# One core: a step's product P moved ahead of its first feed-forward piece, feed-forward input rows read where they were written, guard squares in halves

## Chip, core and metric

The kernel runs on one core of a Trainium2 chip. The metric is the device time of one execution in microseconds (us), median of several runs. A core has five engines that run side by side, each in the order of its own program: TensorE (PE: matmuls into PSUM; PEld is its weight load), VectorE (DVE), ScalarE (ACT), GpSimd (POOL) and SyncE (SP, which here only issues DMAs). They wait for each other through semaphores.

## What is computed

```python
def _attn_ref(r, k, v, w, a, b):          # (4, 8, 768, 40) each: batch, heads, time, width
    state = zeros((B, H, D, D)); y = zeros_like(r)
    for t in range(S):
        y[:, :, t] = einsum('bhd,bhde->bhe', rt, state)
        Sa = einsum('bhde,bhe->bhd', state, at)
        state_decay = state * wt[:, :, None, :] - einsum('bhd,bhe->bhde', Sa, bt)
        state = state_decay + einsum('bhd,bhe->bhde', vt, kt)
    return y

def _moe_ref(x, w_in, w_out):             # x: (3072, 320), w_in: (320, 2048), w_out: (2048, 320)
    r = maximum(x @ w_in, 0.0)
    return (r * r) @ w_out
```

`rt`, `wt` and so on are the rows of time t. The output of the first part, with its heads laid side by side, is the input x of the second. So: a recurrence over 768 time steps for 32 heads of width 40, and a feed-forward layer of 2048 behind it.

## The kernel before

**Tiling.** The recurrence is turned into matmuls over chunks of 128 time steps: 6 chunks (`NCH`), 4 batches (`NB`), 4 pairs of heads a batch (`PB`). One *step* `st` of the main loop handles two pairs (four heads) of one chunk; 8 steps make a chunk (`NQ`), 48 the whole (`NS`), and the loop has two more to drain. Two steps with consecutive numbers, even and odd, share one batch `m`. Steps of a chunk with q = 0 to 3 and 4 to 7 are the two halves (`hf`) of a chunk.

**One step** works on two steps' data at a time, since the results of step st-1 are finished in step st. In its order on TensorE:
- `st_ex_mm(st-1)` (tile ex) and `st_a_mm(st+1)` (tile ca);
- `st_z(st-1)` (tile uy, part from the state of the chunk before, through UBD);
- `st_p(st)` (tile P): ScalarE copies it out as Mc (`st_m`); `st_corr` multiplies Mc back into P, VectorE forms c (`st_c1`), `st_corr` again, and ScalarE writes the result into EVX (`st_sn`, line 296), followed by the guard square jk; GpSimd forms x and Cc;
- `st_t(st, st-2)` (tile tb): transposes that result (VectorE copies it to SnT) and a piece of the next chunk's state (ScalarE copies it to UBD);
- `st_kb(st-1)` fills uy, which `st_y` turns into the output rows YS and the state UZ in the next step.

P and tb have one PSUM buffer between them (tag `sp`, one buffer), so P of a step cannot be written before both SnT and UBD of the step before have been read out of tb.

**Preparations** of a batch m (casts, the decay cs with GI and Gp, and transpositions t1, t2, t3 with their copies RV, KBT, GT and AT) hang in slots of the loop: `prepare(st, 1)` and `prepare(st, 4)`. Even steps have GT and AT of one batch and lnW and the casts of another in slot 1, and cs, GI, Gp, Kp, Bp in slot 4; odd steps RV in slot 1 and KBT in slot 4. `prepare(st, 5)` issues the loads of a batch, six DMAs on SP. Preparations end with step 44; UBD is written for steps 2 to 41.

**Feed-forward.** Each half chunk gives 256 rows of x. `gather` collects them from YS (two heads to a column block, head 2p in partitions 0 to 39 and head 2p+1 in 64 to 103) into three tiles X of 120, 120 and 80 partitions, with eight DMAs. Then there are 12 *pieces*: eight `ffn_in` (two of the 16 blocks of 128 hidden units each: six matmuls into hp, a Relu on ScalarE to hs, a square on VectorE or GpSimd to Gt) and four `ffn_out` (eight matmuls each into an op tile, two pieces to an output tile osb). `filler(st)` runs one piece at each of three places in a step, when it is due; the last ones run behind the loop. hp, op, t1, t2, t3 and cs share two PSUM buffers (tag `ff`).

**Guards.** Squares of some tiles are summed into ACC (jk each step; jm twice at the end of a chunk, over Mc and Cc). If a sum is out of bounds, a slow general path at the end is taken; here it isn't.

**Order.** Each engine's order is the order in which the code calls it; nothing reorders it. The loop body up to the last filler:

```python
filler(st)
if st >= 2:
    st_y(st - 2)
if 1 <= st <= NS:
    st_ex_ev(st - 1)
    st_z(st - 1)
if st < NS:
    st_p(st)
    st_m(st)
prepare(st, 1)
```

Of the kernel before, what the change touches and what calls it, by code (L numbers as in the profile page):

```python
# [7 lines left out]
FP32 = mybir.dt.float32  # L8
BF16 = mybir.dt.bfloat16
# [9 lines left out]
def kernel(  # L19
# [68 lines left out]

    NACC = NS + 2 * NCH + 2 * NBC
    AN, AM, AC, AG, AI = 0, NS, NS + NCH, NS + 2 * NCH, NS + 2 * NCH + NBC
    ACC = gl.tile([128, NACC], FP32, name="ACC")
    ones_f = gl.tile([128, 128], FP32, name="ones_f")
    nc.gpsimd.memset(ones_f[:], 1.0)
# [196 lines left out]
    def st_sn(st):  # L292
        c, q = divmod(st, NQ)
        P, EVX, c1, CN = Ps.pop(st), EVXs[st % NEV], c1s.pop(st), CNs.pop(st)
        Sn = EVX[:, :, :, L + LV:2 * LV].rearrange("p i s e -> p (i s) e")
        nc.scalar.activation(out=Sn, in_=P[:].rearrange("p i s e -> p (i s) e")[:, :, 0:D],  # L296
                             func=ACTF.Copy, scale=-1.0)
        t_ = qdp.tile([128, 4, D], FP32, name="x1", tag="x1")
        nc.gpsimd.tensor_tensor(out=t_[:], in0=Mc[c][:, q], in1=c1[:], op=ALU.add)  # L299
        nc.gpsimd.tensor_tensor(out=Cc[c][:, q], in0=t_[:], in1=Sn, op=ALU.add)  # L300
        jk = qdp.tile([128, 2, 2, L], BF16, name="jk", tag="jk", bufs=1)
        nc.scalar.activation(out=jk[:], in_=CN[:, :, :, 1, :], func=ACTF.Square,  # L302
                             accum_out=ACC[:, AN + st:AN + st + 1])
        if q == NQ - 1:
            for src, at in ((Mc.pop(c), AM), (Cc.pop(c), AC)):
                jm = qdp.tile([128, NQ, 4, D], BF16, name="jm", tag="jm", bufs=1)
                nc.scalar.activation(out=jm[:], in_=src[:], func=ACTF.Square,  # L307
                                     accum_out=ACC[:, at + c:at + c + 1])

    def st_t(st, su):  # L310
        tb = ps.tile([128, 4, 128], BF16, name="tb", tag="sp")
# [61 lines left out]
    def st_y(st):  # L373
        c, o, j0, p2, EVX = where(st)
        uy = uys.pop(st)
        if st % NQ == 0:
            YSs[c] = chp.tile([128, NP, L], BF16, name="YS", tag="YS")
        nc.vector.tensor_tensor(out=YSs[c][:, p2, :], in0=uy[:, :, 0:L],  # L378
                                in1=o.GT[:, j0:j0 + 2, 0:L], op=ALU.mult)
        if c + 1 < NCH:  # L380
            gl_ = o.GT[:, j0:j0 + 2, L:L + 1]
            for u in range(2):
                nc.vector.tensor_tensor(
                    out=UZs[(c + 1) % 2][half(u), p2, 64 * u:64 * u + D],
                    in0=uy[half(u), :, L:LV],
                    in1=gl_[half(u)].to_broadcast([64, 2, D]), op=ALU.mult)

    Xs, Gts, WIN = {}, {}, []  # L390
    rows = [3 * D, 3 * D, 2 * D]
    WOUT = gl.tile([128, NJ, DM], BF16, name="WOUT")
    for g in range(3):
        WIN.append(gl.tile([128, DFF], BF16, name=f"WIN{g}"))

    def load_win():
        off = 0
        for g in range(3):
            nc.gpsimd.dma_start(out=WIN[g][0:rows[g], :], in_=moe_w_in[off:off + rows[g], :])
            off += rows[g]  # L400

    def load_wout():
        nc.gpsimd.dma_start(out=WOUT[:], in_=moe_w_out.rearrange("(j p) f -> p j f", p=128))

    def gather(c, hf, engines):
        X = Xs[c, hf] = [chp.tile([128, HB, L], BF16, name=f"X{g}", tag=f"X{g}")
                         for g in range(3)]
        for h in range(NHH):
            g, row, s = h // 3, (h % 3) * D, h % 2
            src = YSs[c][64 * s:64 * s + D].rearrange("e (b p) t -> e b p t", b=NB)  # L410
            engines[h % len(engines)].dma_start(
                out=X[g][row:row + D], in_=src[:, HB * hf:HB * hf + HB, h // 2, :])

    later = []

# [4 lines left out]
    def ffn_in(c, hf, jj):  # L420
        flush()
        if jj == 0:
            Gts[c, hf] = chp.tile([128, NJ, HB, L], BF16, name="Gt", tag="Gt")
        hp = ps.tile([128, 2, HB * L], FP32, name="hp", **where_ff())
        for u in range(2):
            j = 2 * jj + u
            for g in range(3):
                nc.tensor.matmul(out=hp[:, u, :], lhsT=WIN[g][0:rows[g], j * 128:(j + 1) * 128],  # L428
                                 rhs=Xs[c, hf][g][0:rows[g]].rearrange("p a b -> p (a b)"),
                                 start=(g == 0 and u == 0), stop=(g == 2),  # L430
                                 skip_group_check=True)
        hs = ffp.tile([128, 2 * HB * L], BF16, name="hs", tag="hs")
        nc.scalar.activation(out=hs[:], in_=hp[:].rearrange("p u x -> p (u x)"), func=ACTF.Relu)  # L433
        eng = nc.gpsimd if jj % 2 and not tail else nc.vector
        Gt = Gts[c, hf]
        later.append(lambda: eng.tensor_tensor(  # L436
            out=Gt[:, 2 * jj:2 * jj + 2].rearrange("p j a b -> p (j a b)"),
            in0=hs[:], in1=hs[:], op=ALU.mult))
# [27 lines left out]
    def filler(st):  # L466
        if fill and fill[0][0] <= st:
            fill.pop(0)[1]()
# [8 lines left out]
    def prepare(st, lot):  # L477
        for f, m in when.pop((st, lot), []):
            f(m)
# [6 lines left out]
    for st in (-2, -1):  # L486
        prepare(st, 1)
        prepare(st, 4)
    nc.gpsimd.memset(UZs[1][:], 0.0)
    for st in range(NS + 2):  # L490
        if 1 <= st <= NS:
            st_ex_mm(st - 1)
        if st + 1 < NS:
            st_a_mm(st + 1)
        filler(st)
        if st >= 2:
            st_y(st - 2)
        if 1 <= st <= NS:
            st_ex_ev(st - 1)
            st_z(st - 1)  # L500
        if st < NS:
            st_p(st)
            st_m(st)
        prepare(st, 1)
        if st < NS:
            st_corr(st, Mc[st // NQ][:, st % NQ], False)
            st_c1(st)
        if st + 1 < NS:
            st_a_ev(st + 1)
        filler(st)  # L510
        if st < NS:
            st_corr(st, c1s[st], True)
            st_sn(st)
        filler(st)
        prepare(st, 4)
        st_t(st, st - 2)
        if 1 <= st <= NS:
            st_kb(st - 1)
        if st == 1:
            load_win()  # L520
        if st == 4:
            load_wout()
        if st >= 2:
            c, q = divmod(st - 2, NQ)
            hf = q // (NQ // 2)
            if q % (NQ // 2) == NQ // 2 - 1:
                gather(c, hf, [nc.sync] if st < NS + 1 else [nc.sync, nc.gpsimd, nc.sync])
                at = st + (3 if c + 1 < NCH else 2)
                fill += [(at, lambda c=c, hf=hf, j=j: ffn_in(c, hf, j)) for j in range(NJ // 2)]
                fill += [(at, lambda c=c, hf=hf, b_=b_, p_=p_: ffn_out(c, hf, b_, p_))  # L530
                         for b_ in range(HB) for p_ in range(2)]
        prepare(st, 5)
        if st == 3:
            nc.gpsimd.memset(UZs[0][:], 0.0)
# [9 lines left out]
    nc.vector.memset(ok[:], 1.0)  # L544
    nc.vector.tensor_scalar(out=ok[:, AN:AN + NS], in0=es[:, AN:AN + NS], scalar1=0.75,
                            scalar2=None, op0=ALU.is_le)
    nc.vector.scalar_tensor_tensor(out=ok[:, AM:AM + NCH], in0=es[:, AM:AM + NCH],
                                   scalar=2.0 ** -16, in1=es[:, AC:AC + NCH],
                                   op0=ALU.mult, op1=ALU.is_ge)
    nc.vector.tensor_scalar(out=ok[:, AG:NACC], in0=es[:, AG:NACC], scalar1=2.0 ** 100,  # L550
                            scalar2=None, op0=ALU.is_le)
# [19 lines left out]
    def general():  # L571
# [36 lines left out]
        for bb in range(NB):  # L608
            with tc.For_i(0, T, L) as t0:
                xg = fb.tile([128, NHH, D], FP32, name="xg")  # L610
                nc.sync.dma_start(
                    out=xg[:], in_=ydr[bb, :, bass.ds(t0, L), :].rearrange("h t e -> t h e"))
                xT = fb.tile([128, 3, L], BF16, name="xT")
                xf = xg[:].rearrange("p h e -> p (h e)")
                hp = ps.tile([128, L], FP32, name="hp", tag="ff", bufs=2)
                for g in range(3):
                    nc.tensor.transpose(out=hp[0:rows[g], :],
                                        in_=xf[:, 3 * D * g:3 * D * g + rows[g]], identity=IDf[:])
                    nc.vector.tensor_copy(out=xT[0:rows[g], g, :], in_=hp[0:rows[g], :])
                gt = fb.tile([128, NJ, L], BF16, name="gt")  # L620
                hs = fb.tile([128, L], BF16, name="hb")
                for j in range(NJ):
                    for g in range(3):
                        nc.tensor.matmul(out=hp[:], lhsT=WIN[g][0:rows[g], j * 128:(j + 1) * 128],
                                         rhs=xT[0:rows[g], g, :], start=(g == 0), stop=(g == 2))
                    nc.scalar.activation(out=hs[:], in_=hp[:], func=ACTF.Relu)
                    nc.vector.tensor_tensor(out=gt[:, j, :], in0=hs[:], in1=hs[:], op=ALU.mult)
                op_ = ps.tile([128, DM], FP32, name="op_", tag="ff", bufs=2)
# [39 lines left out]
```

## Time and profile before

| | |
|---|---|
| median of 3 runs | 330.63 us (330.14 to 330.99) |
| the profiled execution | 330.49 us, its span 328.8 us |
| busy in the span: PE, PEld, DVE, ACT, POOL | 280.4, 213.3, 222.7, 232.8, 188.3 us |
| mean granted clock of TensorE | 0.943 |
| first-layer matmuls (L428) | 576, mean 275 ns |
| hs, Relu of 128x512 on ScalarE (L433) | 96, mean 597 ns |
| jm, square of 128x1280 on ScalarE (L307) | 12, mean 1264 ns |
| X from YS (L411) | 96 DMAs of 20 KB, 93 on SP and 3 on GpSimd |
| WIN from HBM (L399) | 3 DMAs on GpSimd, 6.3 us (two) and 9.5 us to landing |
| WOUT from HBM (L403) | 1 DMA on GpSimd, 13.3 us to landing |

The span is what lies between the first and the last instruction of the profiled execution; 1.7 us of its time lie around it. A step's beginning can be read off the first matmul of ex: steps 1 to 9 begin at 25.07, 30.06, 34.90, 38.72, 44.54, 49.81, 54.77, 58.59 and 67.47 us, step 17 at 115.54, 25 at 163.50, 33 at 211.47, 41 at 259.43 and 48 at 296.97. The last eight first-layer pieces start at 310.21.

Timeline rows below show: start, duration, engine and line, operation, output<-inputs and shape, number of instructions merged, and in brackets the idle time of the engine before them with what ended it. The ends of matmuls are modelled; starts are what can be relied on, so spacings from one start to the next are used.

### The profile page before, as it was taken

Reading aid. Unit: us, or ns where it says so; the run is one execution under the profiler, and the core shown is the slowest. Engines: PE = TensorE matmul, PEld = TensorE weight load, DVE = VectorE, ACT = ScalarE, POOL = GpSimd, SP = SyncE. Lnnn points to the kernel's source line nnn. Section 1 sums busy time; section 2 is a strip of 40 time slices with the busy share of each in tenths; the row PEclk is TensorE's granted clock in tenths of the full one; section 3 lists DMA queues with packets and bytes.
Section 4 is the critical chain, followed back from the end, with each engine's and each line's share of the span. In section 5 each row is a group of like instructions: output and inputs, shape, how many; then the busy total and the mean of one; then the engine's idle time right before and its main releaser. Section 6 shows DMA issues by size and latency. Waiting matters only on the chain.

```text
span 328.8 us, 10009 instructions
## 1 busy us (share of the span) xinstructions
PE 280.4 (85%) x3856; PEld 213.3 (65%) x3856; DVE 222.7 (68%) x545; ACT 232.8 (71%) x569; POOL 188.3 (57%) x342
## 2 busy tenths in 40 slices
PE   4478777799999799999799999899998899888990
PEld 3446555577777577777577777677776677666770
DVE  7226968587787587786686886686876775954430
ACT  3366766886886986887986787886887886538450
POOL 3367757296585485676476676476674673533300
PEclk9555978899999999999999999999999999999997
DMA  8992999985737437635736844735862701000100
GB/s 136 174 165 40 176 165 167 169 126 99 151 71 138 94 69 141 126 69 112 128 55 121 147 82 78 144 62 120 131 106 47 147 18 44 20 23 28 55 22 29
DMA packets 164187, 32.86 MB, mean 100 GB/s; under 512 B 158660, under 2 KB 163780, under 8 KB 164130
## 3 DMA queue, kind: packets, MB, share of 16 engines
q1 hardware_dynamic: 161586, 29.44, 49.7%
q0 software_dynamic: 2544, 2.68, 5.1%
q8 instruction: 32, 0.52, 0.7%
q14 instruction: 25, 0.20, 0.2%
HBM read 28.84 MB, written 3.93 MB: 100 GB/s over the span
## 4 chain that ended last, share of the span: by engine, by line
PE 56%; ACT 18%; issue 7%; DVE 7%; POOL 4%; DMA 3%; SPq 3%; ACTq 0%; DVEq 0%; POOLq 0%
PE hp L428 12%; PE t L197 6%; PE ex L341 4%; PE P L280 4%; PE cs L179 4%; ACT hs L433 3%; ACT jm L307 3%; PE uy L368 3%; ACT RV L204 3%; SPq L81 3%; PE tb L316 3%; PE ca L242 2%; DMA NV<-in_v_dram 2%; DVE c L288 2%; ACT GT L224 2%
## 5 line engine op out<-in xcount | busy, mean ns | idle before, releaser
L428 PE MATMUL hp<-X,WIN 120*128 120x256 bf16 (+1 forms) x576 | 78.9, 275 | 8.1 <-ACT osb L458 6.1
L433 ACT ACTIVATE hs<-hp 128x512 bf16<-128x512 f32 x96 | 57.3, 597 | 26.1 <-PE hp L428 22.7
L349 DVE TENSOR_TENSOR EVX<-ex,MEX 128x512 bf16<-128x512 f32 x96 | 61.8, 686 | 1.7 <-PE ex L341 0.5
L428 PEld LDWEIGHTS <-WIN 120*128 120x128 bf16 (+1 forms) x576 | 50.7, 98 | 18.9 <-issue 9.6
L250 DVE TENSOR_TENSOR CN<-ca,MCN 128x512 bf16<-128x512 f32 x96 | 61.4, 681 | 0.7 <-PE ca L242 0.7
L299 POOL TENSOR_TENSOR x<-Mc,c 128x160 f32<-128x160 bf16 x48 | 23.3, 486 | 66.7 <-DVE c L288 66.6
L436 POOL TENSOR_TENSOR Gt<-hs 128x512 bf16<-128x512 bf16 x43 | 48.4, 1125 | 9.9 <-ACT hs L433 9.6
L454 PEld LDWEIGHTS <-Gt 128*128 128x128 bf16 x384 | 34.3, 97 | 13.4 <-POOL Gt L436 0.8
L280 PEld LDWEIGHTS <-CN 128*128 128x128 bf16 x384 | 23.2, 98 | 27.2 <-issue 23.6
L326 DVE COPY SnT<-tb 128x256 bf16<-128x256 bf16 x48 | 14.0, 291 | 33.3 <-PE tb L322 27.6
L300 POOL TENSOR_TENSOR Cc<-x,EVX 128x160 bf16<-128x160 f32 x48 | 25.3, 527 | 17.1 <-ACT EVX L296 16.8
L436 DVE TENSOR_TENSOR Gt<-hs 128x512 bf16<-128x512 bf16 x53 | 27.4, 519 | 9.4 <-ACT hs L433 9.2
L225 DVE TENSOR_TENSOR AT<-t,GT 128x512 bf16<-128x512 bf16 x24 | 10.2, 425 | 31.4 <-ACT GT L224 31.4
L302 ACT ACTIVATE jk<-CN 128x512 bf16<-128x512 bf16 x48 | 30.1, 627 | 0.0
L212 ACT ACTIVATE KBT<-t 128x1024 bf16<-128x1024 bf16 x24 | 24.6, 1024 | 6.0 <-PE t L197 6.0
L204 ACT ACTIVATE RV<-t 128x1024 bf16<-128x1024 bf16 x24 | 24.6, 1023 | 5.1 <-PE t L197 3.0
L188 POOL TENSOR_TENSOR Kp<-NK,GI 128x320 bf16<-128x320 f32 x24 | 22.4, 933 | 6.6 <-ACT GI L182 5.6
L280 PE MATMUL P<-c,CN 128*128 128x40 bf16 x192 | 12.4, 181 | 13.5 <-DVE c L288 13.5
L288 DVE TENSOR_TENSOR c<-P,Mc 128x160 bf16<-128x160 f32 x48 | 15.3, 319 | 10.4 <-PE P L280 9.6
L378 DVE TENSOR_TENSOR YS<-uy,GT 128x256 bf16<-128x256 f32 x48 | 20.2, 421 | 1.2 <-PE uy L368 0.8
L242 PE MATMUL ca<-AT,KBT 64*128 64x128 bf16 x384 | 20.0, 228 | 1.2 <-DVE AT L225 1.2
L296 ACT ACTIVATE EVX<-P 128x160 bf16<-128x160 f32 x48 | 14.4, 300 | 8.7 <-PE P L280 8.4
(142 smaller groups left out, 636.6 us busy)
## 6 DMA issues: line engine op xcount, KB each, us to landing
NW<-in_w_dram SPq DMA_DIRECT2D x24, 160.0 KB
NK<-in_k_dram SPq DMA_DIRECT2D x24, 160.0 KB
NB<-in_b_dram SPq DMA_DIRECT2D x24, 160.0 KB
NA<-in_a_dram SPq DMA_DIRECT2D x24, 160.0 KB
NV<-in_v_dram SPq DMA_DIRECT2D x24, 160.0 KB
NR<-in_r_dram SPq DMA_DIRECT2D x24, 160.0 KB
out_dram<-osb SPq DMA_DIRECT2D x24, 160.0 KB
X<-YS SPq DMA_DIRECT2D x93, 20.0 KB
```

Of the source, the lines that this page charges most:

```text
L204: nc.scalar.activation(out=o.RV[:, :, :, 0:L], in_=t1[:], func=ACTF.Copy)
L212: nc.scalar.activation(out=o.KBT[:], in_=t2[:], func=ACTF.Copy)
L242: nc.tensor.matmul(out=ca[s][:, i, u, :], lhsT=o.KBT[half(s), u, j0 + i, :], rhs=o.AT[half(s), j0 + i, :], start=(i == 0 and u == 0), stop ...
L250: nc.vector.tensor_tensor(out=CN[:, :, s], in0=ca[s][:], in1=MCN[:], op=ALU.mult)
L280: nc.tensor.matmul(out=P[:, i, s, 0:D], lhsT=CN[:, i, s, 1, :], rhs=X[:, 2 * i + s], start=False, stop=last, skip_group_check=True)
L300: nc.gpsimd.tensor_tensor(out=Cc[c][:, q], in0=t_[:], in1=Sn, op=ALU.add)
L302: nc.scalar.activation(out=jk[:], in_=CN[:, :, :, 1, :], func=ACTF.Square, accum_out=ACC[:, AN + st:AN + st + 1])
L349: nc.vector.tensor_tensor(out=EVX[:, :, s, 0:2 * LV].rearrange("p i (u x) -> p i u x", u=2)[:, :, :, 0:L], in0=ex[s][:], in1=MEX[:].rearra ...
L428: nc.tensor.matmul(out=hp[:, u, :], lhsT=WIN[g][0:rows[g], j * 128:(j + 1) * 128], rhs=Xs[c, hf][g][0:rows[g]].rearrange("p a b -> p (a b) ...
L433: nc.scalar.activation(out=hs[:], in_=hp[:].rearrange("p u x -> p (u x)"), func=ACTF.Relu)
L436: later.append(lambda: eng.tensor_tensor(out=Gt[:, 2 * jj:2 * jj + 2].rearrange("p j a b -> p (j a b)"), in0=hs[:], in1=hs[:], op=ALU.mult))
L454: nc.tensor.matmul(out=op_[:], lhsT=Gts[c, hf][:, j, b_, :], rhs=WOUT[:, j, :], start=(j == 0), stop=(j == NJ - 1))
```

## The change

1. **Order in a step.** `st_p` and `st_m` stand directly behind `st_ex_mm` and `st_a_mm`, ahead of the first filler, `st_y` and `st_ex_ev`; the filler follows these, and `st_z` the filler. `prepare(st, 1)`, with its transpositions, moves behind the second filler.
2. **Input rows stay in YS.** The feed-forward multiplies YS as it is: three column blocks (pairs 0 to 2) of 128, 128 and 104 partitions. The rows of heads 6 and 7 are moved by four DMAs into the unused partitions 40 to 63 and 104 to 119 of blocks 0 and 1. The rows of WIN are laid out to match: three memsets on VectorE, and ten GpSimd DMAs in steps 1, 2 and 3 instead of three in step 1. YS gets a third buffer; X is gone.
3. **Due times.** Pieces of a half chunk are due from st+2 (before: st+3, except in the last chunk). WOUT is loaded in step 5 instead of 4.
4. **Guard squares.** jm is taken over half a chunk (640 columns), one over Mc at st mod 4 = 0 and one over Cc at st mod 4 = 1, behind the third filler; before, both over 1280 columns at a chunk's end.

```diff
+    def st_energy(su):
+        if su < 0 or su % (NQ // 2) > 1:
+            return
+        hc = su // (NQ // 2)
+        c, q = divmod(hc * (NQ // 2), NQ)
+        src, at = ((Mc, AM), (Cc, AC))[su % (NQ // 2)]
+        jm = qdp.tile([128, NQ // 2, 4, D], BF16, name="jm", tag="jm", bufs=1)
+        nc.scalar.activation(out=jm[:], in_=src[c][:, q:q + NQ // 2], func=ACTF.Square,
+                             accum_out=ACC[:, at + hc:at + hc + 1])
...
-            YSs[c] = chp.tile([128, NP, L], BF16, name="YS", tag="YS")
+            YSs[c] = chp.tile([128, NP, L], BF16, name="YS", tag="YS", bufs=3)
...
+    NG = PB - 1
+    ROWS = [128, 128, 64 + D]
+    PLACE = [(p, 64 * s, 2 * p + s, 0, D) for p in range(NG) for s in range(2)]
+    MOVED = [(s, 64 * x + D, 2 * NG + s, (64 - D) * x, n)
+             for s in range(2) for x, n in enumerate((64 - D, 2 * D - 64))]
...
+    def load_win(g):
+        for p, row, h, e0, n in PLACE + MOVED:
+            if p == g:
+                nc.gpsimd.dma_start(out=WIN[p][row:row + n, :],
+                                    in_=moe_w_in[h * D + e0:h * D + e0 + n, :])
...
+    def by_pair(c, hf):
+        return YSs[c][:].rearrange("e (b p) t -> e p b t", b=NB)[:, :, HB * hf:HB * hf + HB, :]
     def gather(c, hf, engines):
-        X = Xs[c, hf] = [chp.tile([128, HB, L], BF16, name=f"X{g}", tag=f"X{g}")
-                         for g in range(3)]
-        for h in range(NHH):
-            g, row, s = h // 3, (h % 3) * D, h % 2
-            src = YSs[c][64 * s:64 * s + D].rearrange("e (b p) t -> e b p t", b=NB)
-            engines[h % len(engines)].dma_start(
-                out=X[g][row:row + D], in_=src[:, HB * hf:HB * hf + HB, h // 2, :])
+        X = by_pair(c, hf)
+        for x, (p, row, h, e0, n) in enumerate(MOVED):
+            src = 64 * (h % 2) + e0
+            engines[x % len(engines)].dma_start(out=X[row:row + n, p], in_=X[src:src + n, h // 2])
...
-            for g in range(3):
-                nc.tensor.matmul(out=hp[:, u, :], lhsT=WIN[g][0:rows[g], j * 128:(j + 1) * 128],
-                                 rhs=Xs[c, hf][g][0:rows[g]].rearrange("p a b -> p (a b)"),
+            for g in range(NG):
+                nc.tensor.matmul(out=hp[:, u, :].rearrange("p (a b) -> p a b", a=HB),
+                                 lhsT=WIN[g][0:ROWS[g], j * 128:(j + 1) * 128],
+                                 rhs=by_pair(c, hf)[0:ROWS[g], g],
...
+    for g in range(NG):
+        nc.vector.memset(WIN[g][:], 0.0)
     for st in range(NS + 2):
         if 1 <= st <= NS:
             st_ex_mm(st - 1)
         if st + 1 < NS:
             st_a_mm(st + 1)
-        filler(st)
+        if st < NS:
+            st_p(st)
+            st_m(st)
         if st >= 2:
             st_y(st - 2)
         if 1 <= st <= NS:
             st_ex_ev(st - 1)
+        filler(st)
+        if 1 <= st <= NS:
             st_z(st - 1)
-        if st < NS:
-            st_p(st)
-            st_m(st)
-        prepare(st, 1)
         if st < NS:
             st_corr(st, Mc[st // NQ][:, st % NQ], False)
             st_c1(st)
         if st + 1 < NS:
             st_a_ev(st + 1)
         filler(st)
+        prepare(st, 1)
         if st < NS:
             st_corr(st, c1s[st], True)
             st_sn(st)
         filler(st)
+        st_energy(st - NQ // 2)
         prepare(st, 4)
...
-        if st == 1:
-            load_win()
-        if st == 4:
+        if 1 <= st <= NG:
+            load_win(st - 1)
+        if st == 5:
             load_wout()
...
-                at = st + (3 if c + 1 < NCH else 2)
+                at = st + 2
```

The guard's sums and bounds and the general path follow the new layout.

## The prediction

> **What bounds the kernel now.** I read the page first (busy shares, clock), then the list of waits, then ScalarE's and TensorE's timelines over single steps.
>
> ```profile
> span 328.8 us, 10009 instructions
> PE 280.4 (85%) x3856; PEld 213.3 (65%) x3856; DVE 222.7 (68%) x545; ACT 232.8 (71%) x569; POOL 188.3 (57%) x342
> PEclk9555978899999999999999999999999999999997
> ```
>
> PE is busiest, but no engine is full. The granted clock is high from slice 8 on (about 66 us), so durations from there on can be used as they stand.
>
> ```profile
> PE P L280 <- DVE c L288: 13.5, 26, 1.3
> PE hp L428 <- ACT osb L458: 6.1, 5, 1.2
> PE P L280 <- ACT Mc L273: 3.9, 17, 0.6
> PE P L258 <- ACT UBD L328: 1.6, 5, 0.8
> PE P L264 <- ACT UBD L328: 0.9, 3, 0.5
> ```
>
> Columns: who waits, for whom, us in total, times, longest. The first three lines (23.5 us) are what the change aims at. The last two are small today because a feed-forward piece and Z stand between the step's start and P.
>
> ```profile
> 187.02 0.41 ACT L328 ACTIVATE UBD<-tb 128x256 bf16<-128x256 bf16 x1
> 188.21 0.60 ACT L433 ACTIVATE hs<-hp 128x512 bf16<-128x512 f32 x1 [0.78 <-PE hp L428]
> 188.70 0.30 ACT L273 ACTIVATE Mc<-P 128x160 bf16<-128x160 f32 x1
> 189.08 1.02 ACT L204 ACTIVATE RV<-t 128x1024 bf16<-128x1024 bf16 x1
> 190.01 0.60 ACT L433 ACTIVATE hs<-hp 128x512 bf16<-128x512 f32 x1
> 190.50 0.30 ACT L296 ACTIVATE EVX<-P 128x160 bf16<-128x160 f32 x1
> 190.69 0.63 ACT L302 ACTIVATE jk<-CN 128x512 bf16<-128x512 bf16 x1
> 191.21 0.20 ACT L302 ACTIVATION_READ_ACCUMULATOR jk<-CN 128x1 f32 x1
> 191.30 0.60 ACT L433 ACTIVATE hs<-hp 128x512 bf16<-128x512 f32 x1
> 191.78 1.03 ACT L212 ACTIVATE KBT<-t 128x1024 bf16<-128x1024 bf16 x1
> 192.68 0.40 ACT L328 ACTIVATE UBD<-tb 128x256 bf16<-128x256 bf16 x1
> ```
>
> This is ScalarE over one whole step: from the end of one UBD to the end of the next 5.65 us, of which 0.78 idle before the first hs and 0.17 before RV. It is almost full, and UBD is always its last work of a step.
>
> ```profile
> 192.28 0.39 PE L242 MATMUL ca<-AT,KBT 64*128 64x128 bf16 x8
> 192.60 0.83 PE L428 MATMUL hp<-X,WIN 120*128 120x256 bf16 x6
> 193.28 0.31 PE L358 MATMUL uy<-RV,UBD 128*128 128x168 bf16 x2
> 193.42 0.23 PE L258 MATMUL P<-UZ,AT 128*128 128x80 bf16 x2
> ```
>
> TensorE is at the next step while UBD still runs (to 193.08). Its piece and Z fill the time; P comes at 193.42. P cannot come before UBD ends: tb, which UBD reads, and P share the one buffer of tag sp.
>
> **The change, part by part.**
>
> *The new order.* P now follows ca directly. So P waits for UBD, and everything of the step hangs on P. I lay out ScalarE from P's first matmul (P = 0), with start-to-start spacings from full-clock rows: Mc starts at 0.39 (151.92 to 152.31); the first piece at 0.18; its hs 0.92 after the piece's start (183.51 to 184.43), so at 1.10. PE: a first-layer piece 0.67, Z 0.15, a correction 0.10, so the second piece starts at 1.10, its hs at 2.02. ScalarE is idle from 0.60 to 1.10 and 1.59 to 2.02; with 0.43 from UBD's end to Mc this is 1.36 per step, against 0.95 in the step shown. From 2.02 on it has no gap. Spacings: hs 0.49, RV 0.93, EVX 0.19, jk with its read 0.61, KBT 0.90, GT 0.50, GI 0.41, Gp 0.41, osb 0.33, UBD 0.40 to its end, lnW 0.37 (0.46 less the usual overlap of 0.09).
>
> *Split squares.* jm of 1280 takes 1.16 to its read, jk of 512 takes 0.52; by line through both a half of 640 takes 0.63, with the read 0.72. Two fall into each four steps, so ScalarE does as much as before (two of 1.35 per eight steps), but in the steps with st mod 4 = 0 and 1, no longer in one lump. The lump's 6.1 us of PE waits goes; its price is in the measured steps below.
>
> The four steps of a half chunk, the end of UBD plus 0.04:
> - st mod 4 = 3 (three first-layer pieces): 2.02 + 0.49 hs + 0.93 RV + 0.19 + 0.61 + 0.49 hs + 0.90 KBT + 0.40 = 6.03, so 6.07.
> - 0 (three first-layer): 2.02 + 0.49 + 0.50 GT + 0.37 lnW + 0.19 + 0.61 + 0.49 + 0.72 jm + 0.41 + 0.41 + 0.40 = 6.61, so 6.65.
> - 1 (two first-layer, one second): 2.02 + 0.49 + 0.93 + 0.19 + 0.61 + 0.72 jm + 0.90 + 0.40 = 6.26, so 6.30.
> - 2 (three second-layer of 1.09): PE: pieces 0.18 to 1.27 and 1.52 to 2.61, then eight transpositions; GT starts 0.64 after these (188.44 to 189.08), at 3.25. + 0.50 + 0.37 + 0.19 + 0.61 + 0.33 osb + 0.41 + 0.41 + 0.40 = 6.47, so 6.51.
>
> Sum 25.53. Before, four steps take 23.98 (ex starts of 67.47 and 259.43 are 32 steps apart: 191.96 / 8). +1.55, eight times: **+12.4**. TensorE would be ready for P at 5.25, 5.39, 5.43 and 6.13 of these steps, so the waits for c and Mc are gone (corrections at 1.00 and 2.24, Mc done at 0.69, c at about 1.7), and their time is given to the wait for UBD. Queued behind that P: the step's pieces, Z, corrections, tb, ex; who waits for those is ScalarE itself.
>
> *Steps 1 to 6, no pieces* (29.7 us, from 25.07 to 54.77). Even ones: P to tb 3.23 before (31.03 to 34.26); c no longer stands behind AT on VectorE, but EVX now stands behind GT and lnW: 2.95. Odd ones: 2.27 before (35.81 to 38.08); EVX now behind RV: 2.67. Three of each, and two half squares in steps 4 and 5: -0.84 + 1.20 + 1.44 = **+1.8**. Steps 7 and 8 took 12.70 (54.77 to 67.47; both squares, a wait of 1.1 for X): now 6.07 + 6.65, **0**.
>
> *Last steps.* From step 42 on there is no UBD, and preparations end. PE sums for steps 41 to 47, with the spacings above: 6.30, 6.06, 5.27, 4.50, 4.90, 4.93, 4.23 = 36.2, against 37.5 (259.43 to 296.97): **-1.4**. Pieces begin at st+2 everywhere, so three more run inside the loop and three fewer behind it: from 296.97 to the last hp x48 at 310.21 was 13.2 with a stall of 1.1 behind jm and 0.5 behind a GpSimd Gt; now five first-layer pieces (3.4), four second-layer (4.4) and some 1.2 of ex, Z, kb: 9.0, **-4.2**.
>
> *Gathers.* Four small DMAs for eight: SP needs 0.77 each and they land in 1.8 to 1.9; from the end of step st to the first piece of st+2 there is a step and more (7 us): 0. If they came late the whole step would stop, since P's step queues behind that piece. Once this may bite: before, the last gather was issued at 55.50 and its piece ran at 61.07, behind the loads; the new one is issued by 52.1 and may land at 57.7, about when step 7 wants it; bounds 0 to +3.7, taken 0, since the row for a quiet queue is 1.9.
> *Moving rows from YS* (two runs of 128): no row has it; P L258 reads two runs of 40, at 0.035 for its 80 columns (193.42 to 193.49 for two), the same 0.44 ns a column as hp; 0. Rows 120, 80 or 128: 274 and 275 ns, 0.
> *WIN.* Three memsets (1024 words each; 0.138 for 96 and 0.192 for 160 give 0.92): 2.8 us on VectorE, which idles 4.11 before AT at 22.53: 0, or up to 2.8 without that cover. Ten GpSimd DMAs for three, 0.64 each: 4.5 us more over steps 1 to 3, where GpSimd idles 0.5 to 1 at a time and Kp is used a step later: 0, at most +2. Spread loads may also free batch 4, held 7.3 us by them: down to -1.
>
> The Trainium skill, DMA: Bandwidth & Descriptors, section Why a DMA increments its semaphore by 16 and not by 1, speaks against the new pieces of WIN: a DMA uses the largest number of engines up to 16 that divides its row count, so 40 rows get 8, where 120 and 80 rows got 15 and 16. An estimate by it: twice the 11 us that the three loads took, landed near 52 instead of 41, still ahead of step 7; the sum would be the same, and no run here shows it yet.
>
> **Sum.** 12.4 + 1.8 + 0 - 1.4 - 4.2 = +8.6 on the profiled execution's 330.49 us (span 328.8 and 1.7 around it): **339.1**. The median, 330.63, is 0.14 above that execution; I leave it.
>
> **Rivals.**
> - *Faster: UBD is not late.* If ScalarE reaches UBD before TensorE wants P, the PE marks hold: 5.25 + 5.39 + 5.43 + 6.13 = 22.2, -1.78 eight times, with the other terms 330.49 - 14.2 - 3.8 = 312.5. For it: ScalarE is only 71% busy, and waits for UBD are 2.5 us today. Against it: the step shown leaves it 0.95 us, and P in front takes that slack away. It decides once four steps take under 24.5, that is if ScalarE is 1.1 earlier per four steps than I have it.
> - *Much slower: the first piece waits for its rows.* Gathers late by 1 us in each of twelve half chunks, or 3.7 once and the clock low for longer (a piece at the low clock took 1.45 at 63.67): 345 to 352. For it: SP's queue was in use without a break around 186. Against: 7 us of room.
> - *No change.* The loop gains what ScalarE loses: four steps at 24.4 to 24.6. Nothing in the rows gives just this.
>
> **How the numbers follow.** Forecast 0.72, faster rival 0.14, much slower 0.10, no change 0.04. Below about 0.3% a difference can't be told from none. The bounds (gather +3.7, memsets +2.8, issues +2, loads -1) and 0.5 us either way on each half chunk (4) give the forecast's own range, 334 to 345. To hold eight in ten it is widened to 332 to 346. Faster 0.15, same 0.03, slower 0.82.
>
> **What would show it.** PE P L259 <- ACT UBD should be the largest of PE's waits, some 20 us or more, at about 0.4 to 1.3 a time; waits for c nearly gone; the wait behind jm gone; ex starts 25.5 apart per four steps; ScalarE without idle from the second hs to UBD. Wrong would be: ex starts under 24.5 apart per four steps, or the first matmul of a half chunk waiting on a DMA.

## The result and the profile after

The changed kernel takes 339.52 us (median of 4 runs, 339.29 to 340.72), against 330.81 us for the kernel before on the same chip: a ratio of 1.0264, 95% interval 1.022 to 1.0308. The forecast was 339.1 us, range 332 to 346. The profiled execution took 339.44 us. Ratios, here and below, leave out executions more than 1.5% above the fastest of their kernel; medians take in all.

First the head of its page: the span, the busy times of the engines, the granted clock in 40 slices, and the shares of the chain that ended last.

```profile
span 337.7 us, 9944 instructions
...
PE 280.1 (83%) x3856; PEld 216.1 (64%) x3856; DVE 222.5 (66%) x547; ACT 234.2 (69%) x593; POOL 185.7 (55%) x348
...
PEclk9557955999999999999999999999999999999997
...
PE 41%; ACT 41%; issue 6%; DMA 3%; SPq 3%; DVE 2%; POOL 2%; ACTq 0%; POOLq 0%
```

In the page of the kernel before, the last of these lines reads:

```profile
PE 56%; ACT 18%; issue 7%; DVE 7%; POOL 4%; DMA 3%; SPq 3%; ACTq 0%; DVEq 0%; POOLq 0%
```

The work is what it was (PE 280.1 us against 280.4, ACT 234.2 against 232.8); the span is 8.9 us longer. What changed is who sets the end: ScalarE has 41% of the chain, before it had 18%, although it is busy for only 69% of the span.

The same kernel's list of waits (who waits for whom: us in total, times, longest):

```profile
PE P L259 <- ACT UBD L334: 19.8, 27, 0.9
...
PE P L281 <- ACT Mc L274: 2.9, 7, 0.5
...
PE P L281 <- DVE c L289: 0.9, 2, 0.6
```

The wait for c has gone from 13.5 to 0.9 us and the one of hp for osb (6.1 us) is no longer in the list. In their place stands P's wait for UBD: 19.8 us, before 1.6.

Its timeline over one step, first TensorE from P to the next P, then the same step on ScalarE (start, duration, engine and line, operation, in brackets the idle time before it and what ended it):

```profile
192.86 0.23 PE L259 MATMUL P<-UZ,AT 128*128 128x80 bf16 x2 [0.62 <-ACT UBD L334]
192.93 0.26 PE L265 MATMUL P<-EVX,CN 128*128 128x40 bf16 x4
193.04 0.82 PE L440 MATMUL hp<-YS,WIN 128*128 128x256 bf16 x6
193.70 0.31 PE L364 MATMUL uy<-RV,UBD 128*128 128x168 bf16 x2
...
198.21 0.39 PE L243 MATMUL ca<-AT,KBT 64*128 64x128 bf16 x8
199.49 0.23 PE L259 MATMUL P<-UZ,AT 128*128 128x80 bf16 x2 [0.90 <-ACT UBD L334]
...
193.23 0.30 ACT L274 ACTIVATE Mc<-P 128x160 bf16<-128x160 f32 x1 [0.42 <-PE P L265]
193.95 0.60 ACT L446 ACTIVATE hs<-hp 128x512 bf16<-128x512 f32 x1 [0.42 <-PE hp L440]
194.88 0.60 ACT L446 ACTIVATE hs<-hp 128x512 bf16<-128x512 f32 x1 [0.33 <-PE hp L440]
195.38 0.59 ACT L225 ACTIVATE GT<-t 128x512 bf16<-128x512 bf16 x1
...
197.49 0.75 ACT L313 ACTIVATE jm<-Mc 128x640 bf16<-128x640 bf16 x1
...
199.03 0.41 ACT L334 ACTIVATE UBD<-tb 128x256 bf16<-128x256 bf16 x1
```

From the second hs (194.88) to UBD ScalarE runs without a gap. TensorE has done ca at 198.6 and stands until UBD ends at 199.44. P then starts, and ScalarE, with nothing left to do, waits 0.42, 0.42 and 0.33 us for P and the first two pieces. Each engine waits for the other once a step: the loop is closed through UBD and P, and neither engine is full.

Where the 8.9 us lie, by the starts of ex (us, before and after):

| stretch | before | after | difference | predicted |
|---|---|---|---|---|
| up to step 1 | 25.07 | 25.37 | +0.3 | 0 |
| steps 1 to 6 | 29.70 | 34.02 | +4.3 | +1.8 |
| steps 7 and 8 | 12.70 | 11.56 | -1.1 | 0 |
| steps 9 to 40 | 191.96 | 203.15 | +11.2 | +12.4 |
| steps 41 to 47 | 37.54 | 36.30 | -1.2 | -1.4 |
| from step 48 on | 31.8 | 27.3 | -4.5 | -4.2 |

### The profile page after: what moved, and what is told of

The parts are those of the page before. It is cut to its first block, busy times and chain, and to the rows that moved or that the text cites. A ratio compares the mean times of both kernels' runs of the same rounds, so it can differ in the third digit from the quotient of the medians.

```text
span 337.7 us, 9944 instructions
## 1 busy us (share of the span) xinstructions
PE 280.1 (83%) x3856; PEld 216.1 (64%) x3856; DVE 222.5 (66%) x547; ACT 234.2 (69%) x593; POOL 185.7 (55%) x348
## 4 chain that ended last, share of the span: by engine, by line
PE 41%; ACT 41%; issue 6%; DMA 3%; SPq 3%; DVE 2%; POOL 2%; ACTq 0%; POOLq 0%
PE hp L440 15%; ACT jk L303 7%; ACT KBT L213 5%; ACT RV L205 5%; PE t L198 5%; ACT hs L446 4%; ACT jm L313 4%; DMA NV<-in_v_dram 3%; SPq L81 3%; ACT UBD L334 3%; PE P L259 3%; ACT lnW L172 3%; ACT GI L183 2%; ACT Gp L185 2%; PE P L281 2%
## 5 line engine op out<-in xcount | busy, mean ns | idle before, releaser
L440 PE MATMUL hp<-YS,WIN 128*128 128x256 bf16 (+1 forms) x576 | 77.3, 271 | 3.4 <-ACT hs L446 2.0
L449 POOL TENSOR_TENSOR Gt<-hs 128x512 bf16<-128x512 bf16 x44 | 45.8, 1040 | 25.9 <-ACT hs L446 25.7
L440 PEld LDWEIGHTS <-WIN 128*128 128x128 bf16 (+1 forms) x576 | 50.9, 96 | 10.8 <-issue 5.0
L301 POOL TENSOR_TENSOR Cc<-x,EVX 128x160 bf16<-128x160 f32 x48 | 23.6, 491 | 49.3 <-ACT EVX L297 48.2
L205 ACT ACTIVATE RV<-t 128x1024 bf16<-128x1024 bf16 x24 | 24.5, 1019 | 8.1 <-PE t L198 8.1
L274 ACT ACTIVATE Mc<-P 128x160 bf16<-128x160 f32 x48 | 14.6, 303 | 20.1 <-PE P L265 20.1
L449 DVE TENSOR_TENSOR Gt<-hs 128x512 bf16<-128x512 bf16 x52 | 22.9, 441 | 6.8 <-ACT hs L446 6.7
L180 PE MATMUL cs<-lnW,UTI 128*128 128x320 f32 x48 | 21.0, 522 | 6.7 <-ACT lnW L172 4.3
L259 PE MATMUL P<-UZ,AT 128*128 128x80 bf16 x80 | 9.4, 198 | 20.3 <-ACT UBD L334 19.8
L225 ACT ACTIVATE GT<-t 128x512 bf16<-128x512 bf16 x24 | 14.3, 597 | 16.1 <-PE t L198 16.1
L281 PEld LDWEIGHTS <-CN 128*128 128x128 bf16 x384 | 21.4, 98 | 5.0 <-issue 4.8
L259 PEld LDWEIGHTS <-AT 128*128 128x128 bf16 x80 | 7.3, 96 | 23.7 <-issue 19.2
```

The lines of the kernel that those rows point to most:

```text
L205: nc.scalar.activation(out=o.RV[:, :, :, 0:L], in_=t1[:], func=ACTF.Copy)
L259: nc.tensor.matmul(out=P[:, i, :, 0:D], lhsT=o.AT[:, j0 + i, :], rhs=UZ[:, p2.start + i, :].rearrange("p (s d) -> p s d", s=2)[:, :, 0:D], ...
L281: nc.tensor.matmul(out=P[:, i, s, 0:D], lhsT=CN[:, i, s, 1, :], rhs=X[:, 2 * i + s], start=False, stop=last, skip_group_check=True)
L440: nc.tensor.matmul(out=hp[:, u, :].rearrange("p (a b) -> p a b", a=HB), lhsT=WIN[g][0:ROWS[g], j * 128:(j + 1) * 128], rhs=by_pair(c, hf)[ ...
L449: later.append(lambda: eng.tensor_tensor(out=Gt[:, 2 * jj:2 * jj + 2].rearrange("p j a b -> p (j a b)"), in0=hs[:], in1=hs[:], op=ALU.mult))
```

## The experiments

Twelve kernels, each timed against the kernel before (medians of 4 executions, of 10 for e5 and e8). "Four steps" is an eighth of the time from the start of step 9 to that of step 41 in the profiled execution; it is 24.00 us in the kernel before, where P waits 2.5 us for UBD.

| run | median us | ratio to before (95%) | four steps us | P waits for UBD us |
|---|---|---|---|---|
| after: the change | 339.52 | 1.0264 (1.022 to 1.0308) | 25.39 | 20.3 |
| e1: the change with the old order | 325.42 | 0.9856 (0.9816 to 0.9896) | 23.59 | 1.7 |
| e2: before with the new order | 350.08 | 1.0597 (1.0551 to 1.0643) | 26.38 | 25.0 |
| e3: after, UBD on VectorE | 319.69 | 0.9692 (0.9646 to 0.9737) | 23.17 | none |
| e4: after, WIN in step 0 | 336.94 | 1.0213 (1.0152 to 1.0274) | 25.39 | 20.8 |
| e5: before, UBD on VectorE | 328.95 | 0.995 (0.9912 to 0.9988) | 23.89 | none |
| e6: after, tb and UBD earlier | 325.44 | 0.9831 (0.9738 to 0.9925) | 23.62 | none |
| e7: after, slot 1 moved back | 334.56 | 1.0145 (1.0074 to 1.0217) | 24.85 | 17.3 |
| e8: before, squares in halves | 325.91 | 0.9885 (0.9848 to 0.9922) | 23.73 | 4.5 |
| e9: e3 and e4 together | 316.61 | 0.9582 (0.9515 to 0.9649) | 23.17 | none |
| e10: e1, UBD on VectorE | 324.14 | 0.9825 (0.976 to 0.989) | 23.48 | none |
| e11: after, each jm twice | 357.95 | 1.0795 (1.0702 to 1.0887) | 27.26 | 37.1 |
| e12: e1, each jm twice | 333.67 | 1.0102 (1.0039 to 1.0164) | 24.34 | 9.4 |

The last column adds the rows of P's two groups of matmuls, the one that reads UZ and AT and the one that reads EVX and CN; "none" means that the list of waits has no such row. Each run is compared with the kernel before on its own chip (median 331.06 us for e1 to e4, 330.48 for e5 to e8, 330.46 for e9 to e12).

### Is it the order? (e1, e2)

e1 puts the loop's order back and keeps all else; e2 puts the new order alone into the kernel before. e1's edit:

```diff
-        if st < NS:
-            st_p(st)
-            st_m(st)
+        filler(st)
         if st >= 2:
             st_y(st - 2)
         if 1 <= st <= NS:
             st_ex_ev(st - 1)
-        filler(st)
-        if 1 <= st <= NS:
             st_z(st - 1)
+        if st < NS:
+            st_p(st)
+            st_m(st)
+        prepare(st, 1)
...
         filler(st)
-        prepare(st, 1)
```

> The changed kernel with the old order of a step (first piece and Z ahead of P, t2 and RV ahead of the first correction), all else of the change kept. Theory (P in front waits for UBD): the UBD wait of 19.8 us goes back to some 2 to 3 us, four steps take 23.3 to 24.0 us, in all 322 to 330 us. Rival (the pieces that read YS, the gathers, the due times or WIN cost the time): four steps stay above 25 us, in all 337 us or more.

> The kernel before with the new order of a step alone (P directly behind ca, Z behind the first piece, t2 and RV behind the second). Theory: four steps take about 25.4 us, P waits 18 us or more for UBD, in all 338 to 343 us (the square of 1280 is still one lump). Rival (the order is neutral, another part costs the time): 331 us or less.

The order it is. Without it the rest of the change is a gain: 325.42 against 331.06 us. With it alone the kernel loses 19.0 us (350.08), more than the 14.1 us that it costs on top of the rest (339.52 less 325.42). e1 went as expected; e2 was expected at 338 to 343 us, so its direction was right and its size wrong. Its TensorE timeline at the end of a chunk shows why:

```profile
112.65 0.39 PE L242 MATMUL ca<-AT,KBT 64*128 64x128 bf16 x8
116.20 0.29 PE L258 MATMUL P<-UZ,AT 128*128 128x80 bf16 x2 [3.16 <-ACT UBD L328]
...
116.46 1.45 PE L428 MATMUL hp<-X,WIN 120*128 120x256 bf16 x6
```

The same stretch in windows (from and to, length, busy us of PE, PEld, DVE, ACT and POOL with their instructions, granted clock, DMA share, GB/s):

```profile
111.80:116.20 4.40, 1.24 (x32) 0.98 (x33) 2.39 (x6) 4.26 (x9) 1.90 (x7) 0.84 0.08 26
116.20:121.70 5.50, 5.50 (x43) 4.22 (x42) 2.28 (x5) 2.71 (x7) 0.48 (x1) 0.50 1.07 183
121.70:126.00 4.30, 4.12 (x66) 3.26 (x66) 3.10 (x9) 3.13 (x11) 3.47 (x5) 1.00 0.19 39
```

In e2 both squares of 1280 columns stand ahead of UBD in one step (on ScalarE they start at 111.83 and 113.28, UBD at 115.77). P waits 3.16 us for it, and after that wait the granted clock is 0.50 for 5.5 us, so a first-layer piece takes 1.45 us where 0.82 is usual. Four steps without the lump take 24.38 us there (5.62 + 6.35 + 6.22 + 6.19, from 69.87 on), so the four lumps between steps 9 and 41 cost 211.03 - 8 x 24.38 = 16.0 us, 4.0 each. In the kernel before the step with the lump takes 7.30 us where its like without takes 5.62: 1.7. So the four lumps cost 4 x (4.0 - 1.7) = 9.2 us more in the new order than in the old one; the halves spare it that, which would explain why order and rest don't add up (19.0 against 14.1).

### Is it the wait for UBD, or ScalarE's amount of work? (e3, e5, e6, e10)

e3 copies UBD on VectorE; e5 and e10 do the same in the old order:

```diff
-            nc.scalar.activation(out=UBD[:, 2 * q:2 * q + 2, :], in_=tb[:, 2:4], func=ACTF.Copy)
+            nc.vector.tensor_copy(out=UBD[:, 2 * q:2 * q + 2, :], in_=tb[:, 2:4])
```

> The changed kernel with UBD copied from tb by VectorE, behind its copy of SnT, instead of by ScalarE. Theory (the chain UBD, P, Mc, first piece closes a loop through ScalarE): P's wait for UBD goes to under 5 us in all, four steps take 22.2 to 23.2 us, in all 313 to 322 us, below both kernels. Rival (ScalarE is simply too full, or P has to wait for tb's readers whichever engine reads): four steps above 24.8 us, in all 335 us or more.

> The kernel before with UBD copied by VectorE instead of ScalarE, nothing else changed. Theory (the wait for UBD is made by the new order; in the old one P waits only 2.5 us for it): gain of 1 to 5 us, in all 326 to 330 us. Rival (taking 16 us of work from ScalarE is worth some 20 us in any order, as it was in the changed kernel): 311 to 318 us.

> The changed kernel with the old order and UBD copied by VectorE. Theory (in the old order P hardly waits for UBD): 1 to 3 us less than the old order alone, in all 322 to 325 us, so that with UBD on VectorE the new order is the better one by 2 us or more. Rival (UBD on VectorE is what matters and the order then makes no difference): 317 to 320.5 us.

e6 takes no work from any engine. It only moves UBD up in ScalarE's order:

```diff
         filler(st)
+        st_t(st, st - 2)
         st_energy(st - NQ // 2)
         prepare(st, 4)
-        st_t(st, st - 2)
```

> The changed kernel with the transpositions tb and the copies SnT and UBD ahead of the guard square and of the preparations of slot 4, so that ScalarE does UBD before jm, KBT, GI and Gp; no work is taken from any engine. Theory (what costs the time is UBD's place as the last of ScalarE's order): P's wait for UBD falls under 6 us, KBT or GI and Gp run while P and the first piece do, tb waits some 0.3 to 0.6 us a step for EVX instead; four steps take 23.3 to 24.5 us, in all 322 to 332 us. Rival (ScalarE's amount of work sets the step, wherever UBD stands): four steps 25.0 us or more, in all 336 us or more.

All four fell where the theory put them (e10's gain over e1, 1.3 us, lies within their intervals). The same 16 us of ScalarE's work are worth 19.8 us in the new order (339.52 to 319.69), but 1.5 in the kernel before and 1.3 in e1. And leaving the work on ScalarE but doing it earlier is worth 14.1 us. So it is neither the amount by itself nor the engine, but the place of UBD at the end of a full stretch, with P right behind. As long as UBD stands there, what stands ahead of it does count (e11, below). (Of e6 only the steps from 9 on are read: in its profiled execution, 329.63 us, steps 1 to 8 took 50.35 us at a lower clock.)

The timeline of e3, VectorE's rows and then TensorE's:

```profile
190.53 0.29 DVE L332 COPY SnT<-tb 128x256 bf16<-128x256 bf16 x1 [1.22 <-PE tb L328]
190.74 0.28 DVE L334 COPY UBD<-tb 128x256 bf16<-128x256 bf16 x1
...
191.00 0.39 PE L243 MATMUL ca<-AT,KBT 64*128 64x128 bf16 x8
191.32 0.25 PE L259 MATMUL P<-UZ,AT 128*128 128x80 bf16 x2
```

VectorE had been idle for 1.22 us there, and UBD is done while ca still runs: P follows ca without a gap. The timeline of e6, ScalarE's rows and then TensorE's:

```profile
193.46 0.40 ACT L334 ACTIVATE UBD<-tb 128x256 bf16<-128x256 bf16 x1
193.73 0.77 ACT L313 ACTIVATE jm<-Mc 128x640 bf16<-128x640 bf16 x1
...
192.55 0.30 PE L322 MATMUL tb<-IDb,EVX 128*64 128x128 bf16 x4 [0.22 <-ACT EVX L297]
...
194.60 0.24 PE L259 MATMUL P<-UZ,AT 128*128 128x80 bf16 x2
195.66 0.26 PE L281 MATMUL P<-Mc,CN 128*128 128x40 bf16 x4
```

jm, GI and Gp now run behind UBD, while TensorE does uy, ex, ca and P. The price is a new wait of tb for EVX, 12.5 us in 26 times.

### Does ScalarE's work lie on the path one to one? (e11, e12)

Each half square is done twice, first without a sum, in the changed kernel and in e1:

```diff
+        nc.scalar.activation(out=jm[:], in_=src[c][:, q:q + NQ // 2], func=ACTF.Square)
         nc.scalar.activation(out=jm[:], in_=src[c][:, q:q + NQ // 2], func=ACTF.Square,
                              accum_out=ACC[:, at + hc:at + hc + 1])
```

> The changed kernel with each guard square of 640 columns done twice on ScalarE (the first without a sum): 24 more instructions of some 0.63 us, two in each four steps. Theory (ScalarE's work from the second hs to UBD is a closed loop with P): each lies on the path in full, four steps 26.4 to 26.8 us, +9 to +11 us in the 32 steps from 9 to 41, in all 349 to 355 us. Rival (ScalarE has idle time to give, or the wait for UBD only hides other waits): under +4 us, in all 339 to 344 us.

> The same 24 more squares in the changed kernel with the old order. Theory (there ScalarE has some slack before P, so only a part lies on the path): +2 to +7 us in the 32 steps from 9 to 41, in all 328 to 333 us. Rival (ScalarE is as much the bound in the old order): +9 us or more, 335 us or more.

ScalarE's timeline in e11:

```profile
208.03 0.75 ACT L313 ACTIVATE jm<-Mc 128x640 bf16<-128x640 bf16 x1
208.81 0.74 ACT L314 ACTIVATE jm<-Mc 128x640 bf16<-128x640 bf16 x1
```

An added square costs 0.78 us, not the 0.63 assumed. The two steps that hold one went from 6.48 and 7.14 to 7.19 and 7.91: +0.71 and +0.77, nearly all of it. Four such steps take 7.19 + 7.91 + 5.41 + 6.35 = 26.86 us, just above the 26.4 to 26.8 expected. Two expectations were missed: steps 9 to 40 took 14.9 us more (218.05 less 203.15) for 9 to 11, and the total was 357.95 us (354.01 to 359.45) for 349 to 355. 24 squares are 0.15 us longer each than assumed, and in two of the eight groups of the profiled execution, the longest of the four, the clock fell (last section), which made them 28.4 us. Without the two falls the 32 steps would be 8 x (26.86 - 25.39) = 11.8 us longer. In the old order the first square of a pair costs its whole length (5.69 to 6.46), the second nothing (6.47 and 6.47): +6.0 us between steps 9 and 41, within 2 to 7; 333.67 us is just above the 328 to 333 expected.

### What else the order moved (e7)

```diff
             st_z(st - 1)
+        prepare(st, 1)
         if st < NS:
             st_corr(st, Mc[st // NQ][:, st % NQ], False)
...
         filler(st)
-        prepare(st, 1)
```

> The changed kernel with the preparations of slot 1 back ahead of the first correction; P stays ahead of the first piece and Z behind it. Theory (ScalarE's loop is closed by UBD, and its idle time while it waits for Mc and the first two hs is what the loop loses): RV or GT fills part of the idle time between Mc and the second hs, four steps 24.0 to 25.0 us, in all 327 to 336 us, with P still waiting for UBD. Rival (the place of the preparations was the cost, not P's): four steps 23.5 us or less and no wait for UBD, in all 325 us or less. Third: nothing changes, 338 to 341 us.

From its list of waits:

```profile
PE P L259 <- ACT UBD L334: 15.6, 27, 0.9
PE P L281 <- DVE c L289: 12.7, 26, 1.3
```

The wait for UBD stays, the one for c is back (slot 1 no longer stands between the two corrections to cover it), and yet four steps are 0.54 us shorter, as the theory expected: on ScalarE RV or GT now runs between the first and the second hs, where the changed kernel has 0.33 us idle; the 0.42 us between Mc and the first hs stay. The whole order costs 1.80 us in four steps (25.39 less 23.59), so most of the loss is P's place and a part that of slot 1.

### The first steps: loads of WIN (e4, e9)

```diff
-        if 1 <= st <= NG:
-            load_win(st - 1)
+        if st == 0:
+            for g in range(NG):
+                load_win(g)
```

> The changed kernel with all ten loads of WIN issued in step 0 instead of steps 1 to 3. Theory (the late part of the spread loads competes with batch 4's loads): step 5 takes 5.2 to 5.6 us instead of 8.8, in all 335.5 to 337 us. Rival (the loss of the first steps is the new order's): step 5 stays above 8 us, in all 339 us or more.

> The changed kernel with both edits together: UBD copied by VectorE, and all loads of WIN issued in step 0. Theory: the two losses are separate, in the loop and in the first steps, so the gains add up to what step 5 lost in the run with UBD on VectorE (7.8 us against 5.3): four steps 23.2 us, step 5 under 6 us, in all 315.5 to 318.5 us. Rival (the first steps are set by ScalarE and PE once UBD is off ScalarE): 319 to 321 us as without the second edit.

Step 5 of after takes 8.76 us (before 5.27). Two rows of its timeline, on GpSimd and on TensorE:

```profile
48.21 0.45 POOL L175 CAST Rp<-NR 128x320 bf16<-128x320 f32 x1 [2.97 <-DMA NR<-in_r_dram]
...
48.72 0.61 PE L198 MATMUL t<-IDb,Rp 128*128 128x128 bf16 x4 [2.49 <-POOL Rp L175]
```

The same cast in the timeline of e4:

```profile
44.36 0.45 POOL L175 CAST Rp<-NR 128x320 bf16<-128x320 f32 x1 [0.39 <-DMA NR<-in_r_dram]
```

R of batch 4 was issued at 38.45 and came at 48.2: 9.7 us, where the median of such loads is 3.7. The last six DMAs of WIN were issued between 37.0 and 41.2. With all ten issued in step 0 R's wait is 0.39 and step 5 takes 5.48 us; the median falls by 2.6 us (the two intervals overlap; the profiled spans differ by 2.5). The other runs support it. With the loads of WIN spread over steps 1 to 3, R of batch 4 took 6.2 to 9.7 us from issue to landing in the seven executions in which it was issued among the last six of them, and 4.2 us in e6, where it was issued ahead of them; with the loads in step 0 it took 3.8 (e4) and 4.0 us (e9). It made TensorE wait 2 us or more in four of these ten (after, e1, e3, e10). e9 adds this edit to e3: step 5 falls from 7.84 to 5.27 us, the median from 319.69 to 316.61. e9 is the fastest version, 4.2% below the kernel before. The head of its page:

```profile
span 314.6 us, 9952 instructions
...
PE 277.0 (88%) x3856; PEld 211.4 (67%) x3856; DVE 223.7 (71%) x587; ACT 222.9 (71%) x553; POOL 188.0 (60%) x348
```

TensorE is busy for 88% of it.

### The squares alone (e8)

The halves of the guard squares, their sums and bounds, in the kernel before, nothing else.

> The kernel before with the guard squares in halves alone. Theory (the lump of two squares of 1280 stops TensorE once a chunk, the halves fit into ScalarE's idle time): the wait of hp for osb of 6.1 us goes, in all 323 to 327 us. Rival (ScalarE has as much to do as before, the halves delay the steps they stand in): 329 to 332 us.

As expected: the wait of hp for osb is gone and the kernel gains 4.6 us. The whole rest of the change, in the old order, gains 5.6 (e1). So rows left in YS, small gathers, due times and WIN together bring about 1 us there, by difference, which the two intervals don't tell from none: in the profiled executions 2.5 us behind step 48 (28.7 against 31.2) and 1.1 between steps 9 and 41 (188.74 against 189.81), less 2.9 that steps 1 to 8 lose (42.74 against 39.86).

## Why the prediction was right, step by step

- **The mechanism** is shown: P behind ca waits for UBD, ScalarE's last work of a step, because tb and P share a buffer (tag `sp` of the kernel). The wait is the largest of TensorE's, 19.8 us at up to 0.9 us a time (predicted some 20 us or more, 0.4 to 1.3). Removing what makes it wait (e3, e6) removes the loss.
- **The main term**, +12.4 us, came as +11.2. From P to P the four steps of the example take 5.97, 6.63, 6.27 and 6.52 us; the sum of ScalarE's spacings gave 6.07, 6.65, 6.30 and 6.51. Only the first is off by as much as 0.10 us. The rest of the difference is a slip: 191.96 / 8 is 24.00, not 23.98, which makes the term 12.3. Adding up start-to-start spacings of the engine that closes the loop was enough.
- **Steps 1 to 6** were mis-sized: +4.3 for +1.8, and the sentence that spread loads may free batch 4, "down to -1", had the wrong sign. R of it was indeed issued 2.9 us earlier (38.45, before 41.34), but it came at 48.2, while the kernel before began to cast it at 45.26; by e4 that costs about 2.6 us. Steps 7 and 8 gave 1.1 back that was not in the sum. Most of it is a matter of counting: 6.07 and 6.65 run from P to P, the table from ex to ex, and by ex the same two kinds of step take 5.42 + 6.36 = 11.78 us later on. These two errors and the main term's nearly cancel, 8.9 us in the span for 8.6 predicted. That the total came so close is partly luck; the main term is not.
- **Last steps and tail**: -1.2 and -4.5 us, for -1.4 and -4.2. Part of the tail hangs on the order: with the old one 28.68 us are left from step 48 on, with the new one 27.3.
- **Costs taken as nothing**: the moved rows in YS are free (mean of a first-layer matmul 271 ns, before 275), and so are the memsets (0.91 us each, in VectorE's idle time). The gathers are not late in this run. Their bound of 0 to +3.7 was worth keeping: in e7 and e9, whose steps 1 to 6 are quicker (30.00 and 28.59 us), the first piece waits 1.1 and 1.7 us for its rows.
- **The estimate for WIN** from the Trainium skill, DMA: Bandwidth & Descriptors, section Why a DMA increments its semaphore by 16 and not by 1 (the largest number of engines up to 16 that divides the rows), was worked out wrongly: 10 divides 40, so by that rule 40 rows get 10 engines, not 8 (for some loads issued from GpSimd, as these are, the page names an exception), and the same estimate gives 1.5 times the 11 us instead of twice, landed near 47 instead of 52. Measured: 3.5 to 7.2 us each, the last issued by 41.2, so landed by 48.4 at the latest; no run shows the number of engines. As said, the pieces don't wait for them; what the estimate left out is what else is in flight then.
- **The faster rival** would have held below 24.5 us for four steps; it was 25.39. Its own price was too good: with no wait for UBD left (e3) four steps take 23.17 us, not 22.2; its list of waits, taken over the whole run, still has cs for AT (4.5 us) and lnW (3.9) and P for Mc (2.9). **The much slower rival** and **no change** are out: TensorE waits for no gathered row, and four steps are not at 24.4 to 24.6.

## What to carry to other kernels

Before a consumer is moved forward, look for who last reads the buffer it needs and where that reader stands in its own engine's order: two engines at 83% and 69% can hold each other up once a step, and here the cure was to move the reader (to another engine, or earlier). Less work ahead of the reader may help too, since added work counted nearly in full (e11), but no run tried it, nor a buffer each for P and tb. In such a loop add up the start-to-start spacings of the engine that closes it; that sum gave the step to within 2%. Before loads are moved to where their issuing engine is idle, look at what else is in flight then: R of batch 4 took 3.8 or 4.0 us without them and 6.2 to 9.7 among them.

## What the runs showed of the hardware

TensorE's granted clock fell after waits of 3.16 us and, at times, of 1.66 us. In e2 P waits 3.16 to 3.18 us for UBD five times; in the 5.5 us behind it the granted clock is 0.69, 0.50, 0.71, 0.69 and 0.69. In e11 P waits 1.66 us nine times; in seven of them the clock stays at 1.00, in two it falls. Two windows of e11, each behind such a wait:

```profile
155.50:160.50 5.00, 4.86 (x72) 4.04 (x71) 2.18 (x6) 3.92 (x9) 3.67 (x6) 1.00 0.05 9
...
182.37:187.37 5.00, 5.00 (x44) 4.03 (x44) 1.85 (x4) 2.50 (x5) 2.49 (x4) 0.66 0.03 6
```

The same place in the step, the same wait, 1.00 and 0.66: 72 matmuls against 44 in 5 us. These figures are averages over a window: in both falls of e11 the clock is 0.50 for 3.4 us (182.8 to 186.2, 264.7 to 268.1) and 1.00 before and behind; in e2 it is 0.50 for 3.4 us four times and for 6.8 us once (114.8 to 121.6). In after, where no wait in the later steps is longer than 0.9 us, the clock stays up. The Trainium skill, TensorE: Matmul & The Clock Gate, section HAM oscillation — how this bites in real kernels, asks for no idle gap above some 3.4 us; here gaps of 3.16 us were always enough and gaps of 1.66 us at times, so by these runs that bound is too high for this loop. Why two of nine, no run settles.
